# First routing of a mixture-of-experts chain on one core: expert numbers per token, prefix sums by a scan, lists in gather form, transposes by row group

## Chip, cores and metric

The kernel runs on one core of a Trainium2 chip. The metric is the device time of the whole program in microseconds (us), lower is better. Engines: PE is TensorE, DVE is VectorE, ACT is ScalarE, POOL is GpSimd, SP is SyncE (it only issues transfers here).

## What is computed

Three layers follow each other. Attention over q, k, v of shape (4, 8, 576, 64): a local part (only keys less than 4 positions away) plus a part on 4-fold averaged positions. Its output, 2304 tokens of 512 numbers, goes through a capacity-limited mixture of 8 experts, and that through a dense two-layer network.

```
logits = x @ w_gate                       # x: (2304, 512), w_gate: (512, 8)
for idx in argsort(-logits.flatten()):    # all (token, expert) pairs, best first
    tok, e = idx // 8, idx % 8
    if assigned[tok] >= 0 or counts[e] >= 288: continue
    assigned[tok] = e; counts[e] += 1
out[assigned == e] = relu(x[assigned == e] @ w1[e]) @ w2[e]
h = out @ w_in
y = (h * tanh(softplus(h))) @ w_out
```

## The kernel before

The attention runs over 16 pairs of heads; its result xT stays on the chip in transposed form. For each of 18 token tiles of 128 tokens and each half of the 512 features, `rmm` (L223) makes one psum tile rp that holds the tokens' rows and partial logits, `rxr` (L231) copies the rows to xr on ScalarE, `rlg` (L236) sums the partial logits on VectorE (lg), and after the second half adds both halves into the logits L (L242). rp comes from a psum pool of one bank ("rw") or, for tile 15 and later in alternation, from another single bank ("pd"). `rst` writes the rows to x_dram, from which they are later gathered. The steps have due times in `TP`; a planner orders each engine's queue by them and by its own estimate of when inputs are there.

The routing is done in eight phases, one for each expert that becomes full in turn (`Router.phase`, L355). A phase takes each token's largest remaining logit, finds the point at which one expert is full by a five-level digit search (counts by TensorE, comparisons by VectorE; L401 to L424), says which tokens that expert gets (`sel`: 18 columns of certain ones and 18 of ties), numbers them by prefix sums over the tokens, and makes the list of their 288 token numbers by 18 accumulating matmuls (`it`, L490). The prefix sums go over three matmuls: `to` (L451) sums each column, its copy `ts` goes to sbuf, and `pp` (L455, L456) adds the sums inside a column and over earlier columns. Which expert a token already has stands as a one-hot row of 8 in `self.AO[:, 0]`; the expert it prefers now is in `self.AO[:, 1]` (`OH`). All small psum tiles of the routing share one bank ("rt").

`FFN.gather` (L647) fetches the 288 rows by three indirect transfers on POOL's queue and stores the list in `ilist` by SP. `FFN.expert` (L658) transposes the rows (`xtp`, L671, in three psum buffers "h"), copies them to xh (L673), and runs the expert's two layers: `hp` (L711) and `ya` (L685 or L634 to L636). From the second phase on the routing runs beside the previous expert: `ORDER` begins with R0 R1 E0, and each step of an expert takes one step of the routing forward.

Of the kernel before, what the change touches and what calls it, by code (L numbers as in the profile page):

```python
# [29 lines left out]
RPD = 15  # L30
# [25 lines left out]
class Attn:  # L56
# [166 lines left out]
    def rmm(self, t, half):  # L223


        rp = self.rp[t, half] = (self.p_pd.tile([128, 2, 136], F32, name="rp", tag="pd") if t >= RPD and (t + half) % 2
                                 else self.p_rw.tile([128, 2, 136], F32, name="rp", tag="rw"))
        for i in range(2):
            self.nc.tensor.matmul(rp[:, i], self.xT[:, 2 * half + i, 128 * (t % 9):128 * (t % 9) + 128], self.a['idg_sb'][:, 2 * half + i], start=True, stop=True)
# [6 lines left out]
    def rlg(self, t, half):  # L236
# [4 lines left out]
        if half == 1:  # L241
            V.tensor_tensor(out=self.a['L'][:, t], in0=self.lg[t][:, 0], in1=self.lg[t][:, 1], op=ALU.add)  # L242
# [4 lines left out]
    def emit(self, nar=None, rload=None):  # L247
# [42 lines left out]
def host_route():  # L290
# [14 lines left out]
class Router:  # L305
    def __init__(self, nc, tc, ctx, a):
# [5 lines left out]
        self.tri = c.tile([128, 164], F16, name="rtri")  # L312
# [7 lines left out]
        self.AO = c.tile([128, 2, 18, 8], F16, name="rAO")  # L320
# [5 lines left out]
        nc.gpsimd.memset(self.AO, 0.0)  # L326
# [28 lines left out]
    def phase(self, k):  # L355
# [9 lines left out]
        A, OH = self.AO[:, 0], self.AO[:, 1]  # L365
# [3 lines left out]
        if not last:  # L369
            m0, sg, key, E = F("m0"), F("sg", I32), F("key", I32), P2("E", BF16)  # L370
# [22 lines left out]
        if not last:  # L393
# [36 lines left out]
            V.tensor_scalar(out=full, in0=fw, scalar1=fm[:, 0:1], scalar2=None, op0=ALU.is_equal)  # L430
# [3 lines left out]
        else:  # L434
            V.tensor_scalar(out=full, in0=self.rem, scalar1=30000.0, scalar2=None, op0=ALU.is_lt)
# [3 lines left out]
        s8 = wk.tile([128, 36, 8], F16, name="s8", tag="s8")  # L439
        V.tensor_tensor(out=s8, in0=self.AO.rearrange("p h c e -> p (h c) e"), in1=row8(full, 36), op=ALU.mult)  # L440
        sf = sm.tile([128, 2, 18], F16, name="sf")
        V.tensor_reduce(out=sf.rearrange("p h c -> p (h c)"), in_=s8, op=ALU.max, axis=AX.X)
        sel = sm.tile([128, 2, 18], F16, name="sel")
        if last:
            V.tensor_tensor(out=sel[:, 0], in0=sf[:, 0], in1=sf[:, 1], op=ALU.add)
# [42 lines left out]
        it = self.psr.tile([3, 96], F32, name="it", tag="rt")  # L488
        for c in range(18):
            nc.tensor.matmul(it, R[:, c, :], oa[c], start=(c == 0), stop=(c == 17))  # L490
        ig = wk.tile([3, 96], F32, name="ig")
        V.tensor_scalar_add(ig, it, 1152.0)
        ii = sm.tile([3, 96], I32, name="ii")
        V.tensor_copy(ii, ig)
        ip = self.psr.tile([96, 3], F32, name="ip", tag="rt")
        nc.tensor.transpose(ip, ig, self.a['ident_sb'][0:3, 0:3])
        idx = self.pk.tile([96, 3], I32, name="idx")
        self.last = V.tensor_copy(idx, ip)
# [5 lines left out]
        if not last:  # L504
# [8 lines left out]
            V.tensor_tensor(out=A, in0=A, in1=ON, op=ALU.add)  # L513
# [85 lines left out]
class FFN:  # L599
# [47 lines left out]
    def gather(self, k, idx, ii):  # L647
# [7 lines left out]
        nc.sync.dma_start(self.a['ilist'][288 * k:288 * k + 288, :].rearrange("(g p) o -> g (p o)", g=3), ii)  # L655
        return rows

    def expert(self, k, rows, exi):  # L658
# [9 lines left out]
        for dc in range(4):  # L668
            t = ps['h'].tile([128, 288], F32, name="xtp", tag="h")
            for g in range(3):  # L670
                nc.tensor.transpose(t[:, 96 * g:96 * g + 96], rows[g][:, 128 * dc:128 * dc + 128], self.a['ident_sb'][0:96, 0:96])  # L671
            if plain:
                (nc.vector.tensor_copy if dc % 2 else nc.scalar.copy)(xh[:, dc], t)  # L673
            else:
                nc.scalar.copy(xh[:, dc], t)
                nc.vector.tensor_tensor(out=xl[:, dc], in0=t, in1=xh[:, dc].bitcast(F32), op=ALU.subtract)
# [248 lines left out]
```

## Time and profile before

| | us |
|---|---|
| median of 3 runs | 910.61 |
| the 3 runs | 904.21, 910.61, 911.26 |
| profiled execution, its own time | 907.74 |
| its span, first to last instruction | 906.0 |
| mean granted TensorE clock, share of 2.4 GHz | 0.968 |
| TensorE busy | 865.2 |
| VectorE busy | 667.6 |
| ScalarE busy | 462.2 |
| GpSimd busy | 141.6 |

The attention takes the time to about 161 us, the experts run to about 490 us, the dense network fills the rest. Busy time of TensorE comes from modelled ends of pipelined matmuls, so it says when the engine had work, not that it ran at its peak. A row of the timeline gives start and duration of an instruction or of several alike behind each other; in brackets how long the engine stood idle before it, and what released it.

### The profile page before, as it was taken

What the parts mean: (1) busy time and instruction counts of PE and PEld (TensorE: products, weight loads), DVE (VectorE), ACT (ScalarE), POOL (GpSimd) and SP (SyncE); (2) the same over time, 40 slices, a digit from 0 to 9 for tenths busy, and PEclk for the clock granted to TensorE, in tenths of its full rate; (3) what the DMA queues carried; (4) which work ended last, traced back from release to release, by engine and by line L of the source; (5) the groups of instructions that cost most, each with busy time, mean ns of one, the idle gap of its engine ahead of it and who ended that gap; (6) DMA issues with size and microseconds to landing.
All of it is one profiled execution on the core that took longest, in us unless ns stands there. A gap on an engine that the chain in (4) does not pass through costs nothing.

```text
span 906.0 us, 17967 instructions
## 1 busy us (share of the span) xinstructions
PE 865.2 (95%) x6691; PEld 733.6 (81%) x6691; DVE 667.6 (74%) x1819; ACT 462.2 (51%) x1136; POOL 141.6 (16%) x203
## 2 busy tenths in 40 slices
PE   5999999479999999999999999999999999999996
PEld 3777877356677777778999999999998989999994
DVE  5789886657788888988663888888887565565655
ACT  3587776001233233333554766666666565555553
POOL 5444430021022010203000000000000011111101
PEclk9699999569999999999999999999999999999998
DMA  8656631234384755649752344443433243333311
GB/s 214 158 161 202 169 106 48 95 121 150 126 265 145 241 173 185 198 161 301 232 188 81 89 117 116 116 116 111 123 94 93 47 117 94 94 93 94 93 47 70
DMA packets 69850, 123.42 MB, mean 136 GB/s; under 512 B 8738, under 2 KB 35618, under 8 KB 69762
## 3 DMA queue, kind: packets, MB, share of 16 engines
q1 hardware_dynamic: 34146, 75.08, 26.7%
q0 software_dynamic: 21984, 28.32, 12.2%
q10 hardware_dynamic: 13632, 18.88, 6.1%
q8 instruction: 52, 0.85, 0.4%
q14 instruction: 36, 0.29, 0.1%
HBM read 98.65 MB, written 23.60 MB: 135 GB/s over the span
## 4 chain that ended last, share of the span: by engine, by line
PE 52%; DVE 25%; ACT 15%; issue 4%; DMA 2%; POOL 1%; SPq 0%; POOLq 0%; DVEq 0%; ACTq 0%
PE hp L711 11%; DVE eu L790 5%; DVE eu L791 4%; ACT eu L787 4%; DVE eu L793 4%; ACT eu L788 4%; PE ya L634 3%; ACT gh L796 3%; PE ya L635 3%; PE ya L636 3%; PE cnt L412 3%; PE pvl L213 3%; PE sp L173 3%; ACT eu L789 3%; DVE gl L797 3%
## 5 line engine op out<-in xcount | busy, mean ns | idle before, releaser
L635 PE MATMUL hm<-Yl,wM_sb 128*128 128x256 f32 x576 | 162.3, 282 | 0.0
L636 PE MATMUL hm<-Yh,wM_sb 128*128 128x256 f32 x576 | 162.3, 282 | 0.0
L634 PE MATMUL hm<-Yh,wM_sb 128*128 128x256 f32 x576 | 161.6, 280 | 0.5 <-issue 0.5
L711 PE MATMUL hp<-xh,w 128*128 128x288 f32 x384 | 117.1, 423 | 0.0
L634 PE MATMUL oa<-wM_sb,gh 128*128 128x512 f32 x288 | 113.4, 394 | 3.7 <-ACT gh L796 1.9
L636 PE MATMUL oa<-wM_sb,gl 128*128 128x512 f32 x288 | 113.7, 395 | 0.0
L635 PE MATMUL oa<-wM_sb,gh 128*128 128x512 f32 x288 | 112.9, 392 | 0.0
L634 PEld LDWEIGHTS hm<-Yh,wM_sb 128*128 128x128 f32 x576 | 108.8, 189 | 3.6 <-issue 0.9
L635 PEld LDWEIGHTS hm<-Yl,wM_sb 128*128 128x128 f32 x576 | 108.8, 189 | 2.8
L636 PEld LDWEIGHTS hm<-Yh,wM_sb 128*128 128x128 f32 x576 | 108.4, 188 | 0.0
L796 ACT CAST gh<-eu 128x512 fp32r<-128x512 f32 (+1 forms) x73 | 44.9, 615 | 112.8 <-DVE eu L793 112.8
L790 DVE SCALAR_TENSOR_TENSOR eu<-eu 128x512 f32<-128x512 f32 (+1 forms) x73 | 50.1, 686 | 63.6 <-ACT eu L789 63.2
L720 ACT ACTIVATE gh<-hp 128x288 fp32r<-128x288 f32 (+1 forms) x64 | 26.2, 410 | 108.5 <-PE hp L711 88.9
L797 DVE TENSOR_TENSOR gl<-eu,gh 128x512 fp32r<-128x512 f32 (+1 forms) x73 | 50.0, 684 | 36.1 <-ACT gh L796 36.0
L711 PEld LDWEIGHTS hp<-xh,w 128*128 128x128 f32 x384 | 65.6, 190 | 12.7 <-ACT xh L673 0.3
L634 PE MATMUL ya<-gh,wbh 128*128 128x288 f32 x224 | 72.5, 332 | 0.0
L635 PE MATMUL ya<-gl,wbh 128*128 128x288 f32 x224 | 67.5, 303 | 0.0
L636 PE MATMUL ya<-gh,wbl 128*128 128x288 f32 x224 | 67.1, 301 | 0.0
L787 ACT ACTIVATE eu<-eu,one_sb 128x512 f32<-128x512 f32 (+1 forms) x73 | 52.3, 716 | 28.1 <-DVE eu L786 27.6
L634 PEld LDWEIGHTS oa<-wM_sb,gh 128*128 128x128 f32 x288 | 54.5, 189 | 13.5 <-ACT gh L796 2.7
L636 PEld LDWEIGHTS oa<-wM_sb,gl 128*128 128x128 f32 x288 | 54.4, 189 | 12.5 <-DVE gl L797 0.9
L635 PEld LDWEIGHTS oa<-wM_sb,gh 128*128 128x128 f32 x288 | 54.6, 189 | 9.2
(184 smaller groups left out, 1895.1 us busy)
## 6 DMA issues: line engine op xcount, KB each, us to landing
n<-in_wM_dram SPq DMA_DIRECT2D x32, 512.0 KB
w<-in_wE_dram SPq DMA_DIRECT2D x56, 256.0 KB
w2r<-in_wE_dram SPq DMA_DIRECT2D x40, 256.0 KB
Yh<-y_dram POOLq DMA_DIRECT2D x18, 512.0 KB, 6.0
Yl<-y_dram POOLq DMA_DIRECT2D x18, 512.0 KB, 4.6
wraw<-in_wE_dram SPq DMA_DIRECT2D x16, 512.0 KB
vw<-in_vw_dram SPq DMA_DIRECT2D x16, 315.0 KB
kT<-in_kT_dram SPq DMA_DIRECT2D x16, 291.0 KB
```

The lines of the kernel that those rows point to most:

```text
L173: self.nc.tensor.matmul(sp[r, u], q[r, 64 * n:64 * n + 64], k[r, 64 * n:64 * n + W], start=False, stop=u == 2)
L634: mm(out, lh, rh, start=first, stop=False)
L635: mm(out, lh, rl, start=False, stop=False)
L636: mm(out, ll, rh, start=False, stop=last)
L711: nc.tensor.matmul(hp, w1[:, 128 * dc:128 * dc + 128], xh[:, dc], start=dc == 0, stop=dc == 3)
L787: nc.scalar.activation(out=u, in_=e, func=AF.Square, bias=one)
L788: nc.scalar.activation(out=r, in_=u, func=AF.Ln, bias=one)
L790: nc.vector.scalar_tensor_tensor(out=u, in0=u, scalar=1.0, in1=r, op0=ALU.add, op1=ALU.mult)
L791: nc.vector.scalar_tensor_tensor(out=u, in0=u, scalar=2.0, in1=r, op0=ALU.subtract, op1=ALU.mult)
L793: nc.vector.scalar_tensor_tensor(out=e, in0=u, scalar=0.5, in1=hp[:, 0:w], op0=ALU.add, op1=ALU.mult)
L796: self.cast = nc.scalar.copy(gh[:, 0:w], e)
L797: self.mark = nc.vector.tensor_tensor(out=gl[:, 0:w], in0=e, in1=gh[:, 0:w].bitcast(F32), op=ALU.subtract)
```

## The change

Five edits. (1) rp of the last two token tiles comes from the banks of the score and transpose pools, and their logits are summed ahead of the copy of their rows. (2) The expert a token has, or prefers, is kept as a number per token (`aid`, `own`, as 8 minus the expert) and no longer as a one-hot row, so that `sel` comes out of comparisons with the full expert's number `fm`. `full` is made later; the copy `m0` of the largest logits goes (L is written by an instruction that adds 0.0). (3) Prefix sums: a scan on VectorE adds up each token partition's columns (`run`), and two matmuls, with a matrix of ones and a strictly lower triangle of minus ones, make `pp`; `to` and `ts` go. (4) In phase 0 the list matmuls are turned round (`oa` is loaded, `R` streamed), so that the list comes out as 96 partitions by 3 and one step writes `idx`; it is stored in `ilist` from there, in pieces of 4 bytes. The other phases keep the old form. (5) The transposes of an expert's rows go by row group: three psum tiles of four 96-column blocks instead of four tiles of 288 columns.

```
     def rmm(self, t, half):
-        rp = self.rp[t, half] = (self.p_pd.tile([128, 2, 136], F32, name="rp", tag="pd") if t >= RPD and (t + half) % 2
-                                 else self.p_rw.tile([128, 2, 136], F32, name="rp", tag="rw"))
+        pool, tag = (self.p_pd, "pd") if t >= RPD and (t + half) % 2 else (self.p_rw, "rw")
+        if t >= 16:
+            pool, tag = (self.p_sc, "sc") if t == 16 else (self.p_tr, "tr")
+        rp = self.rp[t, half] = pool.tile([128, 2, 136], F32, name="rp", tag=tag)
...
-            V.tensor_tensor(out=self.a['L'][:, t], in0=self.lg[t][:, 0], in1=self.lg[t][:, 1], op=ALU.add)
+            V.scalar_tensor_tensor(out=self.a['L'][:, t], in0=self.lg[t][:, 0], scalar=0.0, in1=self.lg[t][:, 1], op0=ALU.add, op1=ALU.add)
...
-                add(k + TP['rlg'], self.rlg, t, h)
+                add(k + (TP['rxr'] - 0.01 if t >= 16 else TP['rlg']), self.rlg, t, h)
...
-    tri = np.zeros((128, 164), f)
-    tri[:, 0:128] = np.triu(np.ones((128, 128), f))
-    tri[0:36, 128:164] = np.triu(np.ones((36, 36), f), 1)
+    tri = -np.tril(np.ones((128, 128), f), -1)
...
-                V.tensor_scalar_add(m0[:, c], m[:, c], 0.0)
-                mi = m0[:, c].bitcast(I32)
+                mi = m[:, c].bitcast(I32)
...
             if k:
-                wm2 = F("wm2")
-                V.scalar_tensor_tensor(out=wm2, in0=self.inact, scalar=100.0, in1=wm, op0=ALU.mult, op1=ALU.add)
-            V.tensor_tensor(out=OH[:, c], in0=w2[:, c], in1=bc8((wm2 if k else wm)[:, c]), op=ALU.is_equal)
+                own = F("own")
+                V.scalar_tensor_tensor(out=own, in0=self.inact, scalar=-100.0, in1=wm, op0=ALU.mult, op1=ALU.add)
+            else:
+                own = wm
+            V.tensor_tensor(out=OH[:, c], in0=w2[:, c], in1=bc8(own[:, c]), op=ALU.is_equal)
...
-            V.tensor_scalar(out=full, in0=fw, scalar1=fm[:, 0:1], scalar2=None, op0=ALU.is_equal)
...
-        s8 = wk.tile([128, 36, 8], F16, name="s8", tag="s8")
-        V.tensor_tensor(out=s8, in0=self.AO.rearrange("p h c e -> p (h c) e"), in1=row8(full, 36), op=ALU.mult)
-        sf = sm.tile([128, 2, 18], F16, name="sf")
-        V.tensor_reduce(out=sf.rearrange("p h c -> p (h c)"), in_=s8, op=ALU.max, axis=AX.X)
         sel = sm.tile([128, 2, 18], F16, name="sel")
...
-            V.tensor_tensor(out=sel, in0=ge, in1=sf[:, 1:2].to_broadcast([128, 2, 18]), op=ALU.mult)
-            V.tensor_tensor(out=sel[:, 0], in0=sel[:, 0], in1=sf[:, 0], op=ALU.add)
+            V.scalar_tensor_tensor(out=sel, in0=own.unsqueeze(1).to_broadcast([128, 2, 18]), scalar=fm[:, 0:1], in1=ge, op0=ALU.is_equal, op1=ALU.mult)
+        V.scalar_tensor_tensor(out=sel[:, 0], in0=aid, scalar=fm[:, 0:1], in1=sel[:, 0], op0=ALU.is_equal, op1=ALU.add)
         s2 = sel.rearrange("p h c -> p (h c)")[:, 0:n]
-        to = self.psr.tile([36, 128], F32, name="to", tag="rt")
-        nc.tensor.matmul(to[0:n], s2, self.one, start=True, stop=True)
-        ts = sm.tile([36, 128], F16, name="ts")
-        V.tensor_copy(ts[0:n], to[0:n])
+        run = sm.tile([128, 36], F16, name="run")
+        V.tensor_tensor_scan(out=run[:, 0:n], data0=self.one[:, 0:n], data1=s2, initial=0.0, op0=ALU.mult, op1=ALU.add)
         pp = self.psr.tile([128, 36], F32, name="pp", tag="rt")
-        nc.tensor.matmul(pp[:, 0:n], self.tri[:, 0:128], s2, start=True, stop=False)
-        nc.tensor.matmul(pp[:, 0:n], ts[0:n], self.tri[0:n, 128:128 + n], start=False, stop=True)
+        nc.tensor.matmul(pp[:, 0:n], self.tri, s2, start=True, stop=False)
+        nc.tensor.matmul(pp[:, 0:n], self.one, run[:, 0:n], start=False, stop=True)
+        V.tensor_scalar(out=full, in0=fw, scalar1=fm[:, 0:1], scalar2=None, op0=ALU.is_equal)
...
         idx = self.pk.tile([96, 3], I32, name="idx")
+        if k == 0:
+            it = self.psr.tile([96, 3], F32, name="it", tag="rt")
+            for c in range(18):
+                nc.tensor.matmul(it, oa[c], R[:, c, :], start=(c == 0), stop=(c == 17))
+            self.last = V.tensor_scalar_add(idx, it, 1152.0)
+            ii = None
+        else:
...
-            V.tensor_tensor(out=A, in0=A, in1=ON, op=ALU.add)
+            na = sm.tile([128, 18], F32, name="na")
+            V.scalar_tensor_tensor(out=na, in0=own, scalar=0.0, in1=ge[:, 0], op0=ALU.max, op1=ALU.mult)
+            V.tensor_tensor(out=aid, in0=aid, in1=na, op=ALU.add)
...
-        nc.sync.dma_start(self.a['ilist'][288 * k:288 * k + 288, :].rearrange("(g p) o -> g (p o)", g=3), ii)
+        to = self.a['ilist'][288 * k:288 * k + 288, :]
+        if ii is None:
+            nc.sync.dma_start(to.rearrange("(g p) o -> p (g o)", g=3), idx)
+        else:
+            nc.sync.dma_start(to.rearrange("(g p) o -> g (p o)", g=3), ii)
...
-        for dc in range(4):
-            t = ps['h'].tile([128, 288], F32, name="xtp", tag="h")
-            for g in range(3):
-                nc.tensor.transpose(t[:, 96 * g:96 * g + 96], rows[g][:, 128 * dc:128 * dc + 128], self.a['ident_sb'][0:96, 0:96])
+        for g in range(3):
+            t = ps['h'].tile([128, 4, 96], F32, name="xtp", tag="h")
+            q = slice(96 * g, 96 * g + 96)
+            for dc in range(4):
+                nc.tensor.transpose(t[:, dc], rows[g][:, 128 * dc:128 * dc + 128], self.a['ident_sb'][0:96, 0:96])
             if plain:
-                (nc.vector.tensor_copy if dc % 2 else nc.scalar.copy)(xh[:, dc], t)
+                (nc.vector.tensor_copy if g == 1 else nc.scalar.copy)(xh[:, :, q], t)
```

## Rows read from the trace of the kernel before

**Rows 1.** The page: busy time, share of the span, instructions of each engine.

```profile
PE 865.2 (95%) x6691; PEld 733.6 (81%) x6691; DVE 667.6 (74%) x1819; ACT 462.2 (51%) x1136; POOL 141.6 (16%) x203
```

**Rows 2.** Stretches: length; PE, PEld, DVE, ACT, POOL busy; PEclk; DMA share; GB/s.

```profile
170.00:180.00 10.00, 4.42 (x60) 3.44 (x58) 6.38 (x37) 0.00 (x0) 0.00 (x0) 0.50 0.01 2
190.00:200.00 10.00, 9.20 (x61) 6.15 (x62) 4.54 (x14) 1.13 (x3) 0.13 (x1) 0.66 0.11 36
210.00:220.00 10.00, 10.00 (x70) 6.86 (x69) 7.61 (x38) 1.95 (x4) 2.64 (x6) 1.00 0.34 113
```

**Rows 3.** Timeline (start us, us, engine, line, operation), last logits of the attention.

```profile
158.57 0.73 PE L229 MATMUL rp<-idg_sb,xT 128*128 128x136 f32 x4 [0.44 <-DVE lg L240]
159.74 0.17 DVE L240 TENSOR_REDUCE lg<-rp 128x8 f32<-128x16 f32 x1 [0.74 <-ACT xr L234]
159.97 0.73 PE L229 MATMUL rp<-idg_sb,xT 128*128 128x136 f32 x4 [0.67 <-DVE lg L240]
```

**Rows 4.** Timeline, the copy m0 of the largest logits.

```profile
161.78 0.17 DVE L377 TENSOR_SCALAR m<-m 128x5 f32<-128x5 f32 x1
```

**Rows 5.** Timeline, end of the first routing's search to its prefix sums.

```profile
177.31 0.15 DVE L429 TENSOR_REDUCE fm<-fw 128x1 f32<-128x8 f32 x1
177.51 0.22 DVE L430 TENSOR_SCALAR full<-fw,fm 128x8 f32<-128x8 f32 x1
180.22 0.19 PE L455 MATMUL pp<-sel,rtri 128*128 128x36 f16 x1 [0.37 <-DVE ts L453]
180.35 0.21 PE L456 MATMUL pp<-rtri,ts 36*128 36x36 f16 x1
180.59 0.19 DVE L462 TENSOR_TENSOR pz<-sel,pp 128x36 f32<-128x36 f16 x1
```

**Rows 6.** Groups of instructions by form, 157 to 200 us: busy us, mean ns.

```profile
L475 DVE SCALAR_TENSOR_TENSOR a<-g,am 128x36 f16<-128x36 f32 x1 | 0.2, 215 | 0.0
L448 DVE TENSOR_TENSOR sel<-sel,sf 128x18 f16<-128x18 f16 x1 | 0.2, 151 | 0.0
```

**Rows 7.** Timeline, the first list.

```profile
183.04 1.60 PE L490 MATMUL it<-cmp,R 128*3 128x96 f16 x18 [1.92 <-POOL R L481]
184.67 0.24 DVE L492 TENSOR_SCALAR ig<-it 3x96 f32<-3x96 f32 x1 [0.51 <-PE it L490]
185.25 0.16 DVE L498 CAST idx<-ip 96x3 int32<-96x3 f32 x1
```

**Rows 8.** Timeline, count matmuls of both routings, and the second routing among the first expert's products.

```profile
169.81 1.12 PE L412 MATMUL cnt<-cmp,rAO 128*8 128x64 f16 x18 [0.60 <-DVE cmp L352]
193.58 2.08 PE L412 MATMUL cnt<-cmp,rAO 128*8 128x128 f16 x18
196.97 0.09 PEld L418 LDWEIGHTS <-rfl 9*128 9x128 f16 x1 [0.61 <-DVE xh L673]
```

**Rows 9.** Timeline, SP's queue behind the first list.

```profile
188.05 0.40 SPq L741 DMA_DIRECT2D ixs<-ilist  x1
199.15 0.35 SPq L702 DMA_DIRECT2D w<-in_wE_dram  x1
```

**Rows 10.** Tile xtp (engine idle until, us, times); timeline at the second expert; ScalarE forms.

```profile
  ACT xh L673: 1.2, 5
...
239.06 0.62 ACT L628 CAST wbh<-w2r 128x512 fp32r<-128x512 f32 x1
...
L204 ACT COPY aT<-trl 70x384 f32<-70x384 f32 x22 | 10.5, 476 | 4.5 <-PE trl L199 4.4
```

**Rows 11.** Timeline, TensorE beside the second routing.

```profile
201.25 1.24 PE L711 MATMUL hp<-xh,w 128*128 128x288 f32 x4
208.76 1.62 PE L711 MATMUL hp<-xh,w 128*128 128x288 f32 x6
210.31 0.23 PE L451 MATMUL to<-ones,sel 128*36 128x128 f16 x1
210.47 0.75 PE L711 MATMUL hp<-xh,w 128*128 128x288 f32 x2
```

More of the change, by code (lines that the diff above doesn't have):

```diff
@@ L311, in __init__ @@
         self.thr = c.tile([128, 128], BF16, name="rthr")
-        self.tri = c.tile([128, 164], F16, name="rtri")
+        self.tri = c.tile([128, 128], F16, name="rtri")
         self.index, self.down, self.up = self.small[:, 0:18], self.small[:, 18:26], self.small[:, 26:34]
@@ L319, in __init__ @@
         self.out = {}
-        self.AO = c.tile([128, 2, 18, 8], F16, name="rAO")
+        self.OH = c.tile([128, 18, 8], F16, name="rOH")
+        self.aid = c.tile([128, 18], F32, name="raid")
         self.inact = c.tile([128, 18], F32, name="rinact")
@@ L325, in __init__ @@
             nc.gpsimd.memset(t, -1.0)
-        nc.gpsimd.memset(self.AO, 0.0)
+        nc.gpsimd.memset(self.aid, 0.0)
         nc.gpsimd.memset(self.inact, 0.0)
@@ L364, in phase @@
         two = lambda t: t.unsqueeze(2).to_broadcast([128, t.shape[1], 2])
-        A, OH = self.AO[:, 0], self.AO[:, 1]
+        OH, aid = self.OH, self.aid
         m, wm, w, w2 = F("m"), F("wm"), B("w"), B("w2")
@@ L369, in phase @@
         if not last:
-            m0, sg, key, E = F("m0"), F("sg", I32), F("key", I32), P2("E", BF16)
+            sg, key, E = F("sg", I32), F("key", I32), P2("E", BF16)
             dg = [F(f"dg{i}", I32) for i in range(len(SH))]
@@ L434, in phase @@
         else:
-            V.tensor_scalar(out=full, in0=self.rem, scalar1=30000.0, scalar2=None, op0=ALU.is_lt)
+            fw = sm.tile([128, 8], F32, name="fw")
+            V.scalar_tensor_tensor(out=fw, in0=self.rem, scalar=30000.0, in1=self.down, op0=ALU.is_lt, op1=ALU.mult)
+            fm = sm.tile([128, 1], F32, name="fm")
+            V.tensor_reduce(out=fm, in_=fw, op=ALU.max, axis=AX.X)
         n = 18 if last else 36
         yield
-        s8 = wk.tile([128, 36, 8], F16, name="s8", tag="s8")
@@ L440, in phase @@
-        V.tensor_tensor(out=s8, in0=self.AO.rearrange("p h c e -> p (h c) e"), in1=row8(full, 36), op=ALU.mult)
-        sf = sm.tile([128, 2, 18], F16, name="sf")
-        V.tensor_reduce(out=sf.rearrange("p h c -> p (h c)"), in_=s8, op=ALU.max, axis=AX.X)
         sel = sm.tile([128, 2, 18], F16, name="sel")
         if last:
-            V.tensor_tensor(out=sel[:, 0], in0=sf[:, 0], in1=sf[:, 1], op=ALU.add)
+            V.tensor_scalar(out=sel[:, 0], in0=own, scalar1=fm[:, 0:1], scalar2=None, op0=ALU.is_equal)
@@ L487, in phase @@
             V.tensor_reduce(out=ct, in_=cn.rearrange("p (c e) -> p e c", e=8), op=ALU.add, axis=AX.X)
[L488 to L496, printed above, removed]
-        idx = self.pk.tile([96, 3], I32, name="idx")
-        self.last = V.tensor_copy(idx, ip)
+        idx = self.pk.tile([96, 3], I32, name="idx")
+        if k == 0:
[5 more added lines that the diff above has]
+        else:
+            it = self.psr.tile([3, 96], F32, name="it", tag="rt")
+            for c in range(18):
+                nc.tensor.matmul(it, R[:, c, :], oa[c], start=(c == 0), stop=(c == 17))
+            ig = wk.tile([3, 96], F32, name="ig")
+            V.tensor_scalar_add(ig, it, 1152.0)
+            ii = sm.tile([3, 96], I32, name="ii")
+            V.tensor_copy(ii, ig)
+            ip = self.psr.tile([96, 3], F32, name="ip", tag="rt")
+            nc.tensor.transpose(ip, ig, self.a['ident_sb'][0:3, 0:3])
+            self.last = V.tensor_copy(idx, ip)
         ex = sm.tile([128, 1], F32, name="ex")
@@ L667, in expert @@
             xl = self.xs.tile([128, 4, 288], F32R, name="xl")
-        for dc in range(4):
-            t = ps['h'].tile([128, 288], F32, name="xtp", tag="h")
-            for g in range(3):
-                nc.tensor.transpose(t[:, 96 * g:96 * g + 96], rows[g][:, 128 * dc:128 * dc + 128], self.a['ident_sb'][0:96, 0:96])
+        for g in range(3):
[3 more added lines that the diff above has]
+                nc.tensor.transpose(t[:, dc], rows[g][:, 128 * dc:128 * dc + 128], self.a['ident_sb'][0:96, 0:96])
             if plain:
-                (nc.vector.tensor_copy if dc % 2 else nc.scalar.copy)(xh[:, dc], t)
+                (nc.vector.tensor_copy if g == 1 else nc.scalar.copy)(xh[:, :, q], t)
             else:
-                nc.scalar.copy(xh[:, dc], t)
-                nc.vector.tensor_tensor(out=xl[:, dc], in0=t, in1=xh[:, dc].bitcast(F32), op=ALU.subtract)
+                nc.scalar.copy(xh[:, :, q], t)
+                nc.vector.tensor_tensor(out=xl[:, :, q], in0=t, in1=xh[:, :, q].bitcast(F32), op=ALU.subtract)
         st = {}
```

## Prediction

> **What bounds the kernel now.** I read the page first: TensorE is busy 95% of the span [rows 1]. The table by stretches then shows where it is not. In 170 to 180 us it is busy 4.42 of 10 us at a granted clock of 0.50, which is the 1.2 GHz level. In 190 to 200 the clock is 0.66 and the busy time 9.20, and from 210 to 220 it is 10.00 at 1.00, the 2.4 GHz level [rows 2]. So the kernel has one hole, from the last logits (about 157 us) to the first expert (about 196 us). In it a chain of short VectorE and TensorE steps runs, each waiting for the one before, and every microsecond taken from that chain comes off the end. After it TensorE is the limit: there only TensorE time counts, and VectorE work is hidden as long as VectorE keeps up (it is busy 7.61 of 10 us in 210 to 220). The timeline of the hole then gives each step a start, and the terms below are differences of such starts.
>
> **Last logits in idle psum banks.** Token tile 14 and 15 of the second half, and 17, share the one bank of "rw". The timeline shows the resulting loop: matmul at 158.57, copy to xr on ScalarE, which the sum lg on VectorE at 159.74 waits for, next matmul at 159.97 [rows 3]. One turn is 159.97 - 158.57 = 1.40 us. With tile 16 in "sc" and 17 in "tr", only 14 and 15 still share a bank, so one of the two turns goes. Taking lg ahead of the copy for 16 and 17 keeps those off the end. Bounds: 0.6 if TensorE's queue puts tiles 16 and 17 behind 15 (two more matmul groups of some 0.5 us each at the end, less the copy), 1.5 if the copy is saved too. I take **1.4**.
>
> **Max taken as it is.** The copy m0 is one VectorE step of 0.17 us on the chain [rows 4]. In its place the sum L is written by another instruction of the same size, at no cost on the chain. **0.2** with its hand-over, bounds 0.1 to 0.25.
>
> **Expert number per token and the scan.** Before, fm at 177.31 leads through full, s, sf, two steps for sel, matmul "to", copy ts, and two matmuls to pz at 180.59: 3.28 us [rows 5]. After, the chain is fm, sel, sel[0], scan, last matmul, pz. Steps: fm to its follower 0.20 (177.51 - 177.31); ge's second half, which is in front, 0.10; sel over 36 elements 0.22 (the row of 36 elements), sel[0] 0.15 [rows 6]; the scan; two hand-overs between engines of 0.06; second matmul to pz 0.24 (180.59 - 180.35). No row shows a scan. The nearest is the other step of 36 elements, 0.215 [rows 6]; a scan can't be shorter than the step of 18 elements, 0.15, and if each element had to wait for the one before it, twice 0.215 = 0.43 is my upper bound. I take 0.25, close to the row of the same size. Sum: 0.20 + 0.10 + 0.22 + 0.15 + 0.25 + 0.12 + 0.24 = 1.28, a saving of 2.00. Against it: the preparation of the second routing (m, w, w2 on VectorE) filled the waits that go, and now falls behind pz between short dependent steps. I charge 0.3 for it. **1.7**, bounds 1.2 to 2.1.
>
> **List in gather form (first routing only).** Before, the 18 list matmuls take 1.60 us from 183.04, ig reads them at 184.67, then come a transpose and idx, done at 185.25 + 0.16 = 185.41 [rows 7]. After, one step from psum writes idx: 0.25 like ig. Saving (185.41 - 184.67) - 0.25 = **0.49**. The matmuls themselves now load 96 columns and stream 3, where they loaded 3 and streamed 96. No row of before has this form. The nearest are 62 ns a piece (the 64-column count matmuls, 18 in 1.12 us) and 130 ns (start to start of the two matmuls for pp, 180.22 to 180.35, whose second weight load could not be drawn ahead): 1.12 to 2.34 us [rows 5, 8]. I leave them at 1.60, in the middle, so the bounds of this part are -0.25 to 0.97.
>
> On this the Trainium skill, "TensorE: Matmul & The Clock Gate", LDWEIGHTS (loading the stationary operand), speaks against the exchange: a weight load costs its columns over 1.2 GHz, so what is saved in streaming is paid in loading. By it 18 loads of 96 columns are an estimated 1.44 us, and the sum would be 0.16 lower. No row here shows such a load.
>
> **List written in 4-byte pieces.** SP issues 288 pieces in place of 3 rows. Behind it in SP's queue stands the read ixs, which waits for the list to land (188.05), and behind that the next weight load at 199.15 [rows 9]. These 11.1 us hide it: nothing if the list lands within that time.
>
> **Row-group transposes.** At the first expert four column tiles shared three psum buffers: the last waits for a copy, stands behind the 18 count matmuls of the second routing (2.08 us), and its copy ends late enough that TensorE sits 0.61 us for it [rows 8]. With three tiles for three row groups all twelve transposes run as rows land, and the only late thing is the copy of the last group. TensorE's work in this stretch stays, only its idle time goes: **0.6**, bounds 0 to 1.5. At the other seven experts, TensorE waited some 1.2 us in all on those copies [rows 10]; but the first product now needs the last copy, not the first. I take nothing there, bounds -3.8 (eight times a 384-element copy of 0.48 us) to +1.2.
>
> **Later routings.** There TensorE is the limit, so "to" counts and the VectorE steps don't. Six products of the first layer start at 208.76; at 0.245 each (1.24 us for four less 0.75 for two, halved) the next would start at 210.23, and it starts at 210.47 with "to" between [rows 11]: 0.24. Each of the eight routings has one, and the first is in the hole: 7 x 0.24 = **1.7**, bounds 0 to 2. Removed s, sf, ts and m0 are hidden under TensorE; the added scan and two short steps too.
>
> **Sum.** 1.4 + 0.2 + 1.7 + 0.49 + 0.6 + 1.7 = 6.1 us. The profiled execution took 907.74, so it becomes 901.6. The median of the runs shown is 910.61, and they reach from 904.21 to 911.26; the mean of these three and the profiled one is 908.4, which less 6.1 is **902.3**, the forecast.
>
> **Rivals.**
> *Part of the gain only* (0.20). The hole shrinks by less, since VectorE's queue order or the list matmuls take some back (1.2 for the chain, 2.34 for the list), and the later "to" matmuls were filling gaps. Then the gain is 1.4 + 0.2 + 1.2 - 0.25 + 0.3 = 2.9 us: 905.5. For it: every queue is ordered anew by the planner. Against: the removed steps stand on the chain by their starts.
> *More than the sum* (0.12). The stretch 190 to 200 runs at 0.66, so some two thirds of it at the lower level [rows 2]. If the transposes without a wait bring the high level back as soon as rows land, the 4.5 us from 192.3 to 196.8 lose half their length: 2.2 us more, 900.1, and with the upper bounds 898.
> *Slower than before* (0.08). The copies at the expert boundaries. ScalarE has other work in its queue there: at 239.06 a cast of 0.62 us stands between two copies [rows 10]. Where it stands in front of the last group's copy, TensorE waits 0.62 + 0.48 = 1.1 us before the first product, eight times 8.8 us: 6.1 less 8.8 is 2.7 us slower, 911. It decides from 6.1/8 = 0.76 us a boundary. Against it: TensorE has the previous expert's second-layer products to put in between.
> *As forecast* 0.60, with 898 to 906 as its own range.
>
> **Chances.** About 1% is what a measurement of this kernel can tell from no change: below 901.5 is faster, over 919.7 slower. Two fifths of the forecast's 0.60 lie below 901.5, and the third case's 0.12 too: 0.36. The slower case lies mostly within 1%; beyond it I leave 0.05. Within 1%: 0.59. The range 895 to 909 takes in the partial gain and most of the larger one.
>
> **What would show it.** In the profile after: the last two turns of [rows 3] become one, and the sum for the last logits ends near 160; from fm to pz about 1.3 us; the list's end to the first gather 0.5 shorter; the first product of the first expert near 191.5 rather than 196; TensorE at 10.00 of 10 at the seven later boundaries; the high clock about 4.4 us earlier. Wrong would be: a scan of over 0.5 us, list matmuls over 2.3, a wait for the last copy at each expert, or a first expert that starts 4 us earlier with the same end, which would mean that something later than the hole sets the time.

## The result, and the profile after

| | before | after |
|---|---|---|
| median of the runs beside each other, us | 909.5 | 915.52 |
| their range, us | 902.24 to 911.26 | 909.66 to 920.25 |
| profiled execution, its own time, us | 907.74 | 919.74 |
| its span, us | 906.0 | 918.0 |
| first gather issued, us | 185.69 | 184.13 |
| first transposition of a row group, us | 189.89 | 196.46 |
| first product of the dense network (tile hm), us | 489.6 | 502.8 |

The changed kernel takes 1.0085 times as long, 95% interval [1.006, 1.0111]: 0.85% slower, where 0.7% faster was forecast. That is within the 1% that the prediction counts as no change, but 6.5 us above the upper end of its range, 909. One more run of the changed kernel took 1377.31 us at a mean granted clock of 0.559 and is left out of every figure here.

The table by stretches of after answers [rows 2] (columns as there).

```profile
170.00:180.00 10.00, 4.84 (x62) 3.74 (x62) 6.49 (x39) 0.00 (x0) 0.00 (x0) 0.50 0.01 3
...
190.00:200.00 10.00, 2.97 (x15) 2.12 (x15) 2.02 (x4) 0.96 (x2) 0.00 (x0) 0.50 0.44 102
200.00:210.00 10.00, 10.00 (x57) 6.39 (x57) 2.33 (x12) 0.82 (x2) 0.00 (x0) 0.71 0.17 54
210.00:220.00 10.00, 10.00 (x73) 6.49 (x72) 6.07 (x39) 0.83 (x3) 0.24 (x2) 1.00 0.35 112
```

From 190 to 200 us TensorE is busy 2.97 us where it was busy 9.20, and the high level of the clock (2.4 GHz, 1.00) is there only from 210 on; 200 to 210 is at 0.71. The hole has grown at its end. The timeline shows by what (start us, us, engine, line, operation, in brackets idle time and releaser):

```profile
184.13 1.26 POOL L660 DMA_INDIRECT xrow<-x_dram,idx  x1 [2.65 <-DVE key L380]
183.87 0.35 SPq L665 DMA_DIRECT2D ilist<-idx  x1
184.41 0.33 SPq L715 DMA_DIRECT2D w<-in_wE_dram  x1
191.39 0.39 SPq L754 DMA_DIRECT2D ixs<-ilist  x1
196.46 1.03 PE L684 MATMUL xtp<-ident_sb,xrow 96*128 96x96 f32 x5 [8.00 <-DMA xrow<-x_dram,idx]
199.88 3.25 PE L724 MATMUL hp<-xh,w 128*128 128x288 f32 x6 [0.57 <-ACT xh L686]
```

The same steps in the kernel before:

```profile
185.28 0.30 SPq L655 DMA_DIRECT2D ilist<-ii  x1
185.69 2.00 POOL L652 DMA_INDIRECT xrow<-x_dram,idx  x1 [2.71 <-DMA w<-in_wE_dram]
189.89 0.74 PE L671 MATMUL xtp<-ident_sb,xrow 96*128 96x96 f32 x3 [1.09 <-DMA xrow<-x_dram,idx]
```

The list is issued at 183.87, and the read ixs that waits for it to land goes out at 191.39: 7.5 us, where [rows 9] show 188.05, 2.8 us after the list's issue there. The rows of the gather, which go through another queue, are late too: TensorE waits 8.00 us for them and starts at 196.46, 12.3 us after the gather's issue; before it was 4.2. The DMA view gives the same from issue to landing (median us):

```profile
xrow<-x_dram,idx POOLq DMA_INDIRECT x3, 11.2
```

and in the kernel before

```profile
xrow<-x_dram,idx POOLq DMA_INDIRECT x3, 3.1
```

3.1 us became 11.2.

The steps that the prediction took off the hole are there. Rows of after that answer to [rows 3, 5, 7]:

```profile
159.16 1.66 PE L231 MATMUL rp<-idg_sb,xT 128*128 128x136 f32 x12
162.40 0.17 DVE L244 SCALAR_TENSOR_TENSOR L<-lg 128x8 f32<-128x8 f32 x1
178.09 0.15 DVE L431 TENSOR_REDUCE fm<-fw 128x1 f32<-128x8 f32 x1
179.12 0.22 DVE L451 TENSOR_TENSOR_SCAN run<-ones,sel 128x36 f16<-128x36 f16 x1
179.62 0.19 DVE L461 TENSOR_TENSOR pz<-sel,pp 128x36 f32<-128x36 f16 x1
182.04 1.60 PE L491 MATMUL it<-R,cmp 128*96 128x3 f16 x18 [1.90 <-DVE cmp L353]
183.68 0.16 DVE L492 TENSOR_SCALAR idx<-it 96x3 int32<-96x3 f32 x1 [0.85 <-PE it L491]
```

Three matmul groups of the last logits stand behind each other at 159.16, the step from fm to pz is 179.62 - 178.09 = 1.53 us, the scan 0.22 us, and the list's matmuls take 1.60 us as before, in the form that loads 96 columns and streams 3. From the first copy into xT, the attention's transposed result, to the first gather's issue it is 152.3 us, and was 156.0: 3.8 us gained, and 8.1 lost right behind.

The experts take longer too. From the first transposition to the first hm it is 306.3 us and was 299.7. TensorE's waits between 195 and 495 us (engine, line, what for, us in total, times, longest), after:

```profile
PE xtp L684 <- DMA xrow<-x_dram,idx: 8.0, 1, 8.0
PE j L420 <- DVE jk L418: 3.8, 3, 1.8
PE ip L503 <- DVE ig L499: 2.7, 1, 2.7
PE hp L724 <- ACT xh L686: 0.6, 1, 0.6
```

and before, where there is one:

```profile
PE j L418 <- DVE jk L416: 1.1, 1, 1.1
```

Without xtp these waits are 7.1 us against 1.1. So the 12.0 us between the two profiled spans come about as: 2.2 by a later start of the attention (31.86 us against 29.64 for that first copy; the other kernels below lie between 29.4 and 31.5 whatever they changed, so I don't count it as an effect of the change), less 3.8 up to the gather, 8.1 from there to the first transposition, 6.6 in the experts, less 1.2 behind them. The profiled execution of the changed kernel (919.74) is among the longest of its runs, so 12.0 is twice the difference of the medians, 6.0.

### The profile page after: what moved, and what is told of

Its sections match the earlier page's. It is cut to its first block, busy times and chain, and to the rows that moved or that the text cites. A ratio compares the mean times of both kernels' runs of the same rounds, so it can differ in the third digit from the quotient of the medians.

```text
span 918.0 us, 17938 instructions
## 1 busy us (share of the span) xinstructions
PE 866.0 (94%) x6682; PEld 739.6 (81%) x6682; DVE 656.3 (71%) x1795; ACT 463.5 (50%) x1134; POOL 145.8 (16%) x203
## 4 chain that ended last, share of the span: by engine, by line
PE 49%; DVE 25%; ACT 16%; DMA 5%; issue 4%; POOL 1%; SPq 0%; POOLq 0%; DVEq 0%; ACTq 0%
PE hp L724 10%; DVE eu L803 5%; DVE eu L804 4%; ACT eu L801 4%; ACT eu L800 4%; DVE eu L806 4%; ACT gh L809 4%; PE ya L642 3%; PE ya L643 3%; PE sp L173 3%; ACT eu L802 3%; PE pvl L213 3%; DVE gl L810 3%; PE cnt L414 3%; PE ya L644 3%
## 5 line engine op out<-in xcount | busy, mean ns | idle before, releaser
L724 PE MATMUL hp<-xh,w 128*128 128x288 f32 x384 | 114.2, 433 | 0.6 <-ACT xh L686 0.6
L724 PEld LDWEIGHTS hp<-xh,w 128*128 128x128 f32 x384 | 70.9, 197 | 18.0 <-ACT xh L686 0.9
L642 PE MATMUL ya<-gh,wbh 128*128 128x288 f32 x224 | 74.9, 334 | 0.0
L644 PEld LDWEIGHTS oa<-wM_sb,gl 128*128 128x128 f32 x288 | 54.0, 188 | 12.3 <-DVE gl L810 0.8
```

The lines of the kernel that those rows point to most:

```text
L642: mm(out, lh, rh, start=first, stop=False)
L644: mm(out, ll, rh, start=False, stop=last)
L724: nc.tensor.matmul(hp, w1[:, 128 * dc:128 * dc + 128], xh[:, dc], start=dc == 0, stop=dc == 3)
```

## Experiments

Marks of all kernels, each from one profiled execution; median and ratio from all runs beside the kernel before on the same chip. The kernels were measured in groups on different chips, and the kernel before beside each; so kernels of two groups are compared by their ratios (0.1% is 0.9 us), and their medians are only a guide.

| kernel | median us | ratio, 95% interval | gather issue to first transposition, us | from there to first hm, us |
|---|---|---|---|---|
| before | 909 to 910 | | 4.2 | 299.7 |
| after | 915.52 | 1.0085 [1.006, 1.0111] | 12.3 | 306.3 |
| after, list in rows | 908.9 | 1.0022 [0.9996, 1.0048] | 4.6 | 306.5 |
| after, pieces issued on POOL | 911.0 | 1.0036 [1.0003, 1.007] | 4.3 | 310.6 |
| before, list in pieces | 911.84 | 1.0044 [1.001, 1.0079] | 9.8 | 302.4 |
| list in rows, column transposes | 906.08 | 0.9967 [0.9936, 0.9998] | 4.5 | 303.5 |
| the same, ip later | 902.93 | 0.9943 [0.9909, 0.9976] | 4.5 | 297.8 |
| the same, ixs late too | 901.25 | 0.9899 [0.9838, 0.9961] | 4.7 | 300.5 |
| the same, row-group transposes | 904.14 | 0.9948 [0.992, 0.9976] | 4.6 | 302.7 |
| column transposes, ip later, ixs late, pieces late | 902.85 | 0.9937 [0.9907, 0.9967] | 5.2 | 296.6 |
| before, row-group transposes | 913.46 | 1.0044 [1.0011, 1.0077] | 4.4 | 303.2 |
| the same, ip later | 914.28 | 1.0043 [1.0006, 1.0079] | 4.4 | 301.1 |

Runs of one kernel differ by some 10 us (before: 901.97 to 912.58). One source can be seen in the two kernels with the list in rows and column transposes, whose TensorE orders are the same in this stretch. The first eight products of the first expert took, with ip (a transposition of the last routing's list, explained below) as the planner had it, and with ip later:

```profile
191.96 4.10 PE L728 MATMUL hp<-xh,w 128*128 128x288 f32 x8
```

```profile
191.46 2.21 PE L730 MATMUL hp<-xh,w 128*128 128x288 f32 x8
```

4.10 us and 2.21 us for the same instructions: in the first kernel the granted clock is 0.50 (1.2 GHz) from 188 to 196 us, in the second it is 1.00 (2.4 GHz) from 191 on, though TensorE was busy without a gap from 188 in both. Why the clock came up at different moments no run shows. A single profile can't tell 2 us.

### The list in rows, and on another queue

Of the changed kernel, the first list alone is undone: one more transposition of the 96 x 3 numbers, and three rows are written. In the second kernel the pieces stay, but POOL issues them, behind the three gathers.

```
-            ii = None
+            ig = wk.tile([96, 3], F32, name="ig0")
+            V.tensor_scalar_add(ig, it, 1152.0)
+            ip = self.psr.tile([3, 96], F32, name="ip", tag="rt")
+            nc.tensor.transpose(ip, ig, self.a['ident_sb'][0:96, 0:96])
+            ii = sm.tile([3, 96], I32, name="ii")
+            V.tensor_copy(ii, ip)
... the second kernel
-            nc.sync.dma_start(to.rearrange("(g p) o -> p (g o)", g=3), idx)
+            nc.gpsimd.dma_start(to.rearrange("(g p) o -> p (g o)", g=3), idx)
```

> The changed kernel, but the first list goes to memory as 3 rows of 384 bytes again: beside idx a second copy of the list is transposed on TensorE and stored from there. All else as changed; the order of the engines' queues is that of the changed kernel. Theory P (the 288 pieces of 4 bytes keep the transfer engines busy, and the gathered rows wait behind them): the first transposes start about 4 us after the first gather is issued, as before (4.2), and not 12.3, so 8 us come off, and some 2.6 more because TensorE leaves the 1.2 GHz level sooner: 905 to 908, ratio to before 0.995 to 0.999. Theory W (two weight loads, which the planner now puts behind the list's store, run beside the gather and hold it up): those loads stay where they are, so no change: 916, ratio 1.008.

> The changed kernel with the same 288 pieces of 4 bytes, but issued on POOL's queue behind the three gathers instead of on SP's ahead of them. Theory P: the rows no longer wait, first transposes about 4 us after the first gather's issue, 905 to 908, ratio 0.995 to 0.999; the pieces still take some 7 us, but nothing needs them then. Theory W: 916, ratio 1.008, since the weight loads stay.

With the list in rows the first transposition comes 4.6 us after the gather's issue:

```profile
181.27 1.15 POOL L665 DMA_INDIRECT xrow<-x_dram,idx  x1 [2.65 <-DVE key L380]
185.84 0.39 PE L689 MATMUL xtp<-ident_sb,xrow 96*128 96x96 f32 x1 [3.82 <-DMA xrow<-x_dram,idx]
```

The median falls by 6.6 us to 908.9, the ratio by 0.63%, which is 5.7 us; by the two intervals it is roughly 2 to 9 us. So the wait that is gone does not all come back: 905 to 908 was expected. One of the two weight loads that stood behind the list in SP's queue still does (issued at 182.23, the list at 181.73), and the rows are on time, so it is the pieces; the loads were not taken away by themselves. Issued on POOL, the pieces come behind the three gathers. The rows of the first two are on time; those of the third, issued 0.9 us ahead of the pieces, are not:

```profile
185.33 0.91 POOL L660 DMA_INDIRECT xrow<-x_dram,idx  x1 [0.30 <-issue]
186.24 0.76 POOL L665 DMA_DIRECT2D ilist<-idx  x1
186.03 0.90 PE L684 MATMUL xtp<-ident_sb,xrow 96*128 96x96 f32 x4
191.94 0.42 PE L684 MATMUL xtp<-ident_sb,xrow 96*128 96x96 f32 x1 [3.53 <-DMA xrow<-x_dram,idx]
```

3.53 us of the loss come back at the third group, and the kernel takes 911.0, again more than the 905 to 908 expected. So moving the pieces to another queue does not make them harmless as long as a gather is under way. The Trainium skill, "DMA: Bandwidth & Descriptors", Issuing engines are not separate DMA queues, says that transfers from all issuers run on the same 16 DMA engines and interleave. The trace of the changed kernel agrees: pieces that SP issued held up rows that POOL issued, 11.2 us in place of 3.1.

### The pieces alone, in the kernel before

```
-        nc.sync.dma_start(self.a['ilist'][288 * k:288 * k + 288, :].rearrange("(g p) o -> g (p o)", g=3), ii)
+        to = self.a['ilist'][288 * k:288 * k + 288, :]
+        if k == 0:
+            nc.sync.dma_start(to.rearrange("(g p) o -> p (g o)", g=3), idx)
+        else:
+            nc.sync.dma_start(to.rearrange("(g p) o -> g (p o)", g=3), ii)
```

> The kernel before with one line changed: the first list is stored from idx in 288 pieces of 4 bytes instead of 3 rows. Queue orders are those of before, all weight loads stand ahead of the store. Theory P: first transposes at about 198 us instead of 190, the whole 8 to 10 us slower than before, ratio 1.008 to 1.011. Theory W: as before, ratio 1.000.

TensorE's and ScalarE's orders are those of before, instruction by instruction; the one write is changed. The rows are late:

```profile
194.49 0.74 PE L675 MATMUL xtp<-ident_sb,xrow 96*128 96x96 f32 x3 [6.65 <-DMA xrow<-x_dram,idx]
```

9.8 us from the gather's issue (184.74) in place of 4.2: the pieces alone delay the rows by 5.6 us. In the changed kernel it was 8.1. There two weight loads stand behind the pieces in SP's queue, and here SP issues nothing else until 192.79; whether the other 2.5 us come from those loads is not shown. The profiled span is 912.2, 6.2 more than before, but the medians differ by only 2.7 (911.84 beside 909.1) and the ratio is 1.0044, 4.0 us, where 8 to 10 were expected; which part of the wait the other executions take back, one profile doesn't show.

### The pieces, written later

List in pieces as in the changed kernel, but issued behind a cast of the first expert, when the first gather's rows have landed (with column transposes and the two moves below).

```
-            nc.sync.dma_start(to.rearrange("(g p) o -> p (g o)", g=3), idx)
+            self.late = (to, idx)
... in expert(), ahead of the push of product j
+            if k == 0 and j == 3:
+                ld = nc.sync.dma_start(self.late[0].rearrange("(g p) o -> p (g o)", g=3), self.late[1])
+                self.tc.add_manual_dep(ld.ins, self.cast.ins.name, mybir.DependencyInfo(mybir.DependencyClass.NoSync, mybir.DependencyReason.DATA), reason="order")
```

> The list in 288 pieces of 4 bytes as in the changed kernel, but written later: on SP behind a cast of the first expert, when no gather is under way; column transposes, ip later and reads ixs late as in the run at 901.25. Theory P2 (the pieces cost because the first gather's rows are in flight beside them): the rows land as with the list in rows, first transposition 4.2 to 4.6 us after the gather's issue, and the kernel takes 900.5 to 902.5. Rival P3 (the pieces cost wherever they stand, since the weight loads then come late): 904 to 909, with TensorE waiting for a weight.

902.85 (0.9937), beside 902.93 (0.9943) and 901.25 (0.9899, 4 runs) for the two kernels with the list in rows: written late, the pieces cost nothing that these runs can tell. The first transposition comes 5.2 us after the gather's issue, where 4.2 to 4.6 was expected. The table by stretches, first of the kernel before (the list, in rows, issued at 185.28), then of the changed kernel (the list issued at 183.87), then of this one (issued at 203.86; columns as in [rows 2]: the last two are the DMA engines' busy share and GB/s):

```profile
186.00:188.00 2.00, 1.28 (x13) 1.28 (x13) 0.84 (x3) 0.00 (x0) 1.70 (x2) 0.50 0.32 115
190.00:192.00 2.00, 1.68 (x8) 0.96 (x8) 1.14 (x3) 0.00 (x0) 0.13 (x1) 0.50 0.53 170
```

```profile
184.00:186.00 2.00, 0.24 (x1) 0.06 (x1) 2.00 (x9) 0.00 (x0) 1.57 (x2) 0.50 0.87 199
186.00:188.00 2.00, 1.62 (x16) 1.62 (x17) 0.57 (x5) 0.00 (x0) 1.70 (x2) 0.50 0.48 27
188.00:190.00 2.00, 0.46 (x5) 0.17 (x2) 0.29 (x2) 0.00 (x0) 0.60 (x1) 0.50 0.29 14
190.00:192.00 2.00, 0.00 (x0) 0.00 (x0) 0.00 (x0) 0.00 (x0) 0.00 (x0) 0.50 0.54 42
194.00:196.00 2.00, 0.00 (x0) 0.00 (x0) 0.00 (x0) 0.00 (x0) 0.00 (x0) 0.50 0.96 251
```

```profile
204.00:206.00 2.00, 2.00 (x24) 1.29 (x23) 0.53 (x3) 0.00 (x0) 0.00 (x0) 1.00 0.79 260
208.00:210.00 2.00, 2.00 (x12) 1.45 (x11) 1.96 (x18) 0.41 (x1) 0.26 (x2) 1.00 0.22 15
210.00:212.00 2.00, 2.00 (x17) 1.35 (x16) 2.00 (x12) 0.00 (x0) 1.49 (x3) 1.00 0.49 9
212.00:214.00 2.00, 2.00 (x20) 1.40 (x17) 1.97 (x10) 0.17 (x1) 0.00 (x0) 1.00 0.61 32
```

In both kernels with pieces the pieces' own packets are over within some 2 to 3 us, and then, for about 6 us, whatever comes behind them creeps: 27, 14 and 42 GB/s in the changed kernel, 15, 9 and 32 in the other, at a busy share of up to 0.61. In the first case it is the gather's rows that creep and TensorE (first column) has nothing to do; in the second it is weights that are needed later, and TensorE is busy throughout at 1.00. It is not that much else is moved then: by the trace's records of single packets, a few of them take very long. Of all packets of 2 KB and more, whose median is 93 ns, none takes 2 us in the whole run of the kernel before; in the changed kernel ten do, all begun between 185 and 192 us, and the longest takes 3.3 us. In the kernel before with pieces the longest takes 3.9 us, in this one 4.0. With the pieces issued on POOL it looks different: there no packet of this stretch takes 1 us, the last packet of the third gather is over at 188.1, and nothing is moved from then until TensorE starts on it at 191.94. Why packets and landings behind a burst of 4-byte writes are so slow, no row shows.

### Column transposes, and ip later

The kernel with the list in rows, with the transposes of before; then the same with five pauses of the last routing's recording ahead of ig, by which the planner puts the transposition ip 78 matmuls later on TensorE, with all else on TensorE in the same order; then the same with the reads ixs issued late.

```
-        for g in range(3):
-            t = ps['h'].tile([128, 4, 96], F32, name="xtp", tag="h")
+        for dc in range(4):
+            t = ps['h'].tile([128, 288], F32, name="xtp", tag="h")
... and so on as before; then, ahead of ig
+            for _ in range(5 if last else 0):
+                yield
... and, at the reads ixs
-            nc.sync.dma_start(ixs, ...)
+            ld = nc.sync.dma_start(ixs, ...)
+            self.tc.add_manual_dep(ld.ins, self.cast.ins.name, mybir.DependencyInfo(mybir.DependencyClass.NoSync, mybir.DependencyReason.DATA), reason="order")
```

> As a_rowlist, but the transposes of the rows go by feature column again (four tiles of 288 columns, four copies), so that the row-group edit alone is undone. If that edit is worth its term of the prediction (0.6 us), this is 0.6 us slower than a_rowlist and the stretch from the first expert to the dense network keeps the 296.6 us that it has in the changed kernel. If the row-group edit is what made that stretch 6.1 us longer than before (290.5), this is 4 to 6 us faster than a_rowlist.

> The changed kernel with the first list in rows and the old column transposes (906.1), and the transposition ip of the last routing put some 64 instructions later on TensorE, behind products that need nothing of it. Theory Q (the 3 us in which TensorE sits for ig at about 419 us, and the 1.6 us that the next eight products then lose at the lower clock, come from where the planner put ip): the stall at 418 to 422 goes, and the kernel is 4 to 4.6 us shorter, 901.5 to 902.5, which is the forecast of the prediction. Rival S (the wait only moves: TensorE sits for VectorE's or ScalarE's work some products later): 905 to 906.5.

> As the run with ip later, and the reads ixs of the list for the last expert's groups, which stand on SP and wait there for the list to land, are issued later, behind the cast of a late product, so that the two weight loads behind them go out sooner and nothing waits on SP in the hole. Theory: the gather's rows land 0 to 0.6 us sooner and the kernel takes 901 to 902.5. Rival (the wait of 2.8 us on SP is covered): the same as the run with ip later, within 0.7 us.

906.08, 902.93, 901.25; as ratios 0.9967, 0.9943, 0.9899. Column transposes are worth 2.8 us beside row groups by the medians (908.9), 5.0 by the ratios (1.0022). The first of the three still has the wait for ip; on ScalarE, VectorE and TensorE:

```profile
416.65 0.62 ACT L641 CAST wbh<-w2r 128x512 fp32r<-128x512 f32 x1 [4.09 <-DMA w2r<-in_wE_dram]
417.30 0.69 DVE L642 TENSOR_TENSOR wbl<-w2r,wbh 128x512 fp32r<-128x512 f32 x1 [3.67 <-ACT wbh L641]
417.91 0.24 DVE L504 TENSOR_SCALAR ig<-it 3x96 f32<-3x96 f32 x1
418.21 0.20 PE L508 MATMUL ip<-ident_sb,ig 3*96 3x3 f32 x1 [2.93 <-DVE ig L504]
418.34 3.25 PE L728 MATMUL hp<-xh,w 128*128 128x288 f32 x6
```

A weight tile w2r is late for ScalarE (4.09 us), whose cast wbh VectorE's wbl waits for (3.67); behind wbl stands ig, which needs nothing of it, and behind ig's transposition on TensorE stand products that need nothing of either. TensorE sits 2.93 us, and the next six products take 3.25 us at a granted clock of 0.57 to 0.58, where eight took 2.10 a little later at 1.00. With ip later that wait is gone from the trace, and the median is 3.1 us lower, less than the 4 us or more that were expected. By the ratios it is 0.24%, 2.2 us, and the two intervals overlap: the wait is shown, a gain of the whole kernel from moving ip is not. Reading ixs late gives 901.25 from 4 runs; that it is better than 902.93 can't be told.

### The row-group transposes

The last kernel with row groups again, and the kernel before with row groups alone, as the planner has it and with ip later.

```
... the kernel before
-        for dc in range(4):
-            t = ps['h'].tile([128, 288], F32, name="xtp", tag="h")
-            for g in range(3):
-                nc.tensor.transpose(t[:, 96 * g:96 * g + 96], ...)
+        for g in range(3):
+            t = ps['h'].tile([128, 4, 96], F32, name="xtp", tag="h")
+            q = slice(96 * g, 96 * g + 96)
+            for dc in range(4):
+                nc.tensor.transpose(t[:, dc], ...)
... and the copies to xh in the same blocks
```

> The kernel before with one edit: the transposes of the gathered rows go by row group in place of by column tile. Theory R (the edit costs time by itself: the first product of an expert now needs the last copy, and the list's order puts count matmuls in between): the first product of the first expert comes 0.5 to 1 us later after the gather's issue than before, and the kernel takes 2 to 3 us more than before, 911 to 912, as the difference of the two runs with the list in rows (908.9 less 906.1). Rival N (that difference was the chance order of those two kernels): within 1 us of before. The prediction's own step says 0.6 us less than before.

> The last run (list in rows, ip later, reads ixs late; 901.25) with the row-group transposes of the changed kernel put back. Theory R2 (the two runs with the row-group transposes lost to the order that the planner made of the later experts, not to the transposes): with ip out of the way, the first product of the first expert starts 0 to 1 us after the third copy, and the kernel takes 900.5 to 902.5. Rival R (waiting for the third copy costs by itself): 2 to 3 us more than the column transposes, 903.5 to 904.5, with TensorE's waits for xh standing at several experts.

> The kernel before with the row-group transposes (913.46) and the transposition ip of the last routing some 50 instructions later. Theory R2 (what that edit lost is the 2.4 us for which TensorE sat for ig, with what the clock then loses): 3.5 to 4.5 us shorter, 909 to 910, within 1 us of the kernel before, and the first expert starts 0.6 to 0.8 us sooner after its gather than before. Rival R: 912 to 913.5.

All the pairs point one way: 2.8 us by the medians (908.9 beside 906.08), 2.9 and 1.2 (904.14 beside 901.25 and 902.93), 3.2 (913.46 beside 910.22), and 914.28 for the last, beside 909.7. The two in the kernel before (ratios 1.0044 and 1.0043, some 4 us) stand clear of noise, and the intervals of the first pair (1.0022 and 0.9967) hardly touch; 904.14 (0.9948) can't be told from 0.9899 or 0.9943. So the expectation that the edit is free once ip is out of the way is not borne out: in the kernel before it still costs 0.43%. The first form of the theory against it, that the wait for the third copy costs by itself, fell too: in the kernel before with row groups the first product starts 9.5 us after the gather's issue and not 10.3, so its start gains 0.8. The loss lies in the middle of the expert stage. TensorE waits for jk, a step of the next routing's search on VectorE; with row groups (ip later) and with columns:

```profile
PE j L420 <- DVE jk L418: 4.4, 3, 1.9
```

```profile
PE j L420 <- DVE jk L418: 2.2, 2, 1.9
```

One of the three waits with row groups, at 342 us, has this chain:

```profile
340.15 0.62 ACT L643 CAST wbh<-w2r 128x512 fp32r<-128x512 f32 x1 [2.45 <-DMA w2r<-in_wE_dram]
341.32 0.69 DVE L611 TENSOR_TENSOR wM_sb<-nt,wM_sb 128x512 fp32r<-128x512 f32 x1 [2.64 <-ACT wM_sb L610]
341.93 0.27 DVE L418 TENSOR_SCALAR_CACHE_REDUCE jk<-cnt 8x128 f16<-8x128 f32 x1
342.27 0.17 PE L420 MATMUL j<-reye,rfl 9*128 9x8 f16 x1 [1.91 <-DVE jk L418]
```

Again a weight w2r is late for ScalarE, its cast wbh holds up the cast wM_sb behind it, VectorE's step on wM_sb waits for that (2.64 us), and jk stands behind it. With column transposes the planner has jk ahead of wM_sb at this place, and TensorE doesn't wait. In the kernel before with row groups alone it is the wait at 263 us, 2.1 us (2.6 with ip later) in place of 1.1. These waits are 1 to 2 us of each pair's difference. The clock adds something behind some of them (in the kernel before with row groups it is at 0.50 from 264 to 266 us) and nothing behind others (1.00 from 342 to 348 us, behind the chain above). The rest stays open, and so does why moving ip, which took 2.4 us of waiting out of that kernel's trace, did not lower its median (913.46, 914.28): its profiled execution (908.71) lies at the lower end of its runs and doesn't show what the others lose.

## Why the prediction was wrong

**Up to the gather it was right, as far as one profile of each kernel shows.** Last logits: 1.2 us gained (3.13 from the last copy into xT to the last sum, was 4.31), 1.4 forecast. From the first largest logits to the step g it is 17.88 us, was 19.90: 2.0, with m0 in it, 1.9 forecast. From fm to pz it is 1.53 us; 1.28 and a charge of 0.3 were taken. The scan takes 0.22 (0.25 was taken). Turning the list round gains 0.56 (0.49), and the list matmuls stay at 1.60, where they were left. Together 3.8 us, as the first four terms of the sum say. On the list matmuls the Trainium skill ("TensorE: Matmul & The Clock Gate", LDWEIGHTS) gave an estimated 1.44; the measurement decides: 1.60, as with the operands the other way round.

**The step that failed: "These 11.1 us hide it: nothing if the list lands within that time."** It priced the 4-byte pieces by who stands behind the list in SP's queue. There the argument holds, for the list lands in 7.5 us, within the 11.1. But the gather's rows, in POOL's queue, were moved beside it and held up (11.2 us in place of 3.1), and they were the next thing that TensorE needed. The term was 0 and measured 5.7 us by the ratios, 6.6 by the medians (915.52 less 908.9); without it the changed kernel can't be told from the kernel before (908.9, [0.9996, 1.0048]) and lies inside the prediction's range, at its upper end. The rival that forecast a slower kernel had the direction by another mechanism, the wait for the last copy at each expert, which the next paragraph looks for. The prediction asked which instruction waits for the transfer, and not which transfers run beside it.

**Row groups: the wrong place was watched.** At the first expert the term of 0.6 came out as 0.8 in the kernel before, in part by luck: the 0.61 us of [rows 8] is idle time of the weight loads (PEld), during which TensorE's matmuls ran on by the profile, and what went were three shorter gaps between the transpositions (0.26, 0.38 and 0.17 us). Of the waits for the last copy at every expert, which the slower rival was made of, the trace of after has one, 0.57 us at the first. What the edit costs, 3 to 5 us where it stands clear of noise, was not priced. Of this 1 to 2 us are traced: the planner, with another order of the copies, puts jk behind a step that waits for a weight. The rest is open.

**Later routings: the gain is not shown, and new waits outweigh it.** The eight "to" matmuls are gone; with the waits for ip and the row groups taken out, the expert stage is 296.6, 297.8 and 300.5 us in three profiles, on average 1.4 below the 299.7 of before. The forecast was 1.7, but the three lie 3.9 us apart, so the agreement may be luck. In the changed kernel as it stands the stage takes 306.3, with 7.1 us of waits in place of 1.1. The prediction said that TensorE is the limit there, so that the matmul counts and the VectorE steps don't: it counted VectorE as hidden by its busy share, though in these traces it stalls TensorE where a short step of the routing stands behind a step that waits for a weight.

**The sum in the end.** With the list in rows, column transposes and ip later the kernel takes 902.93, or 0.9943 of the kernel before: 5.2 us less, 2 to 8 by the interval. The terms of the edits that are left come to 5.5 (6.1 without the 0.6 of the row groups). So those edits can hold what was forecast for them, though the runs don't tell it term by term. What ate it in the changed kernel is the transfer priced at 0, the row groups, and perhaps the order that puts ip in TensorE's way: 1.42% of ratio together, some 13 us. The version with the lowest median, 901.25 [0.9838, 0.9961], beats both kernels.

## What to carry to other kernels

Price a transfer by what else is in flight while it runs, on all queues, and not only by what waits for it: here a kilobyte in 4-byte pieces was dear while the next thing needed was on its way, and 20 us later it cost nothing that could be told. Where a planner orders the queues, each edit also reorders work that it doesn't touch, so look in the new trace for short steps that stand in an in-order queue behind one that waits for a load; one such step held TensorE for 2.9 us, half of what the whole change was to bring. And a busy share of 76% (7.61 of 10 us in [rows 2]) is no sign that an engine keeps up: what counts is where its waits stand.

## What the hardware showed that was not expected

A burst of 288 writes of 4 bytes is soon through by its own packets, but for about 6 us after it the transfers behind it moved at 9 to 42 GB/s in the changed kernel and in the one that writes the list late, where the kernel before moved 115 to 170 behind its list (10 to 76 with the pieces put into it, from 186 to 194 us). Single packets of 2 KB and more, 93 ns in the median, then took up to 3.3 and 4.0 us, and rows of a gather that landed in 3.1 us took 11.2. Issued on POOL's queue, the pieces still held up the third gather's rows, by 3.53 us. And the same eight products, in the same order, took 2.21 or 4.10 us, by the moment at which the granted clock came up.
